# A place of its own for the second half of batch 1's v, loaded together with the first half

## The chip, the cores and the metric

The kernel runs on one core of one Trainium2 chip. The metric is the device time of one execution in microseconds (us), as the median of several runs; a profile records one execution more closely, engine by engine: PE (TensorE, matrix products), DVE (VectorE), ACT (ScalarE), POOL (GpSimd, which here mostly issues weight loads) and SP (SyncE, which issues the other loads and the stores).

## The reference

The inputs are q, k and v of 8 batches, 8 heads, 576 rows, 64 columns, and two weight matrices. A linear attention (softmax of q over its columns, softmax of k over the sequence) is followed by two matrix products with a gate between:

```
q_s = softmax(q, axis=-1);  k_s = softmax(k, axis=2)
kv  = einsum('bhsd,bhse->bhde', k_s, v)
x   = einsum('bhsd,bhde->bhse', q_s, kv)      -> 4608 x 512
h   = x @ w_in                                # 512 x 2048
g   = h * erf(softplus(h))
out = g @ w_out                               # 2048 x 512
```

The weights arrive as 64-bit floats, are read as 32-bit integers, and are decoded by shifts and masks on DVE.

## The kernel before, in words

**Tiling.** Two batches make a pair of 1152 tokens, which is cut into three blocks of 384 tokens. For each block and each of four groups of 512 hidden columns there is a work item n: up-matmuls (`mm1_32` for the first six items, in 32-bit; `mm1` later, with operands split into two 16-bit parts), softplus and erf on ACT, the multiplication `gmul` on DVE, and out-matmuls `mm2` on PE that accumulate over the groups. In the profile the up-matmuls of the first items are line L1031 (banks pX, pY, pZ), the first out-matmuls L1109 (o), the later ones L992 and L1118.

**Attention.** `attention(b)` is a generator for batch b, from batch 1 on; the order string `ORDER` and later `pace` take its pieces (token A) between the pieces of the work items. For one batch: maximum of k and its transposes (kT L524, kB L539), exponentials of k and q (L349), then two products `kv_mm(b, 0)` and `kv_mm(b, 1)` (L560, the name kv), one for each half of four heads. Each multiplies a half of k with the same half of v, and with the 64 tail rows of k and v (`kt`, `vtail`). A column of ones beside v gives the sum of k's exponentials, and `kv_norm` (L580 to L583) divides by it on DVE. `kv_max` (L589) takes the largest value, which PE turns (x_bk, L125) and DVE reduces (x_e, L127) to a scale. Then come the normalisation of q, its transposes (qT, L657) and the product x (L675).

**Where v lies.** `vbuf` holds one half of v, of four heads. `load_kv(b)` loads both halves of k, and the first half of v into vbuf, then `vtail`; for b > 0 the second half is loaded into the same vbuf (L415, called in `attention` at L714), once `kv_mm(b, 0)` has read it. SP issues its DMAs strictly in its written order, so whatever stands behind one that waits, waits too. Batch 0 is treated by itself in `start`: its second half of v lies in a buffer of the work items (tag G).

**Where the weights lie.** `WT` is a list of eight places, one for each slab of w_in or w_out in the order of `JOBS`. In the end a place holds the split 16-bit operands; for w_in it has 7168 16-bit columns. Before that, the first 4096 columns of a place serve as a landing place of raw weight pieces (`wload`, L188) and as the place of a decoded slab (`wdecode`, L214 shift, L217 and L220 or). WT[0], the first place for w_in's operands, is a landing place again and again until all pieces are decoded; its split operands are written by `wsplit(0)` (token S0), after the pieces of batch 1's attention. The first eight raw pieces are issued by SP, the other eight by POOL, each when DVE's last decoding step of an older piece has freed the landing place (rw or WT[0], WT[1]).

The written order is that in which the code calls things; the layer that records the program then places each engine's instructions, and may let some pass others. The order of the program on each engine, as it was built, is what the rows of order below show.

Of the kernel before, what the change touches and what calls it, by code (L numbers as in the profile page):

```python
# [9 lines left out]
F32 = mybir.dt.float32  # L10
# [46 lines left out]
def attn_moe_kernel(  # L57
# [9 lines left out]
    nc = tc.nc  # L67
    B, H, S, D = q.shape
# [4 lines left out]
    TM = 4  # L73
# [41 lines left out]
    WT = [  # L115
        cp.tile([P, 2 * (7 if which == "in" else 4) * 512], F16, name=f"wt{i}")
        for i, (which, g) in enumerate(JOBS)
    ]
# [283 lines left out]
    def load_half(src, tag, b, hf):  # L402

        s4 = src[b, hf * 4:hf * 4 + 4, 0:SM, :].rearrange("h (p t) d -> p h t d", t=TM)
        if tag == "v" and b == 0 and hf == 1:
            t = ch.tile([P, 4, TM, D + 1], F32, tag="G", bufs=2, name=f"v_{b}_{hf}")
            nc.gpsimd.memset(t[:, :, :, D:], 1.0)
        elif tag == "v":
            t = vbuf
        else:  # L410
            t = at.tile([P, TM, 4, D], F32, tag=tag, name=f"{tag}_{b}_{hf}")
        eng = nc.sync
        for h in range(4):
            o = 2 * (h % 2) + h // 2 if tag == "q" else h
            eng.dma_start(t[:, h, :, :D] if tag == "v" else t[:, :, o, :], s4[:, h])  # L415
        return t
# [9 lines left out]
    def load_tail(src, tag, p):  # L426
        t = at.tile([P, H, D], F32, tag=tag, bufs=1, name=f"{tag}_{p}")
        for j in range(2):
            nc.sync.dma_start(
                t[j * TAIL:(j + 1) * TAIL],  # L430
                src[2 * p + j, :, SM:S, :].rearrange("h p d -> p h d"),
            )
        return t

    def load_vtail(b):

        j = b % 2
        own, rest = (slice(i * TAIL, (i + 1) * TAIL) for i in (j, 1 - j))
        nc.gpsimd.memset(vtail[rest], 0.0)
        nc.gpsimd.memset(vtail[own, :, D:], 1.0)  # L440
        nc.sync.dma_start(
            vtail[own, :, :D], v[b, :, SM:S, :].rearrange("h p d -> p h d")
        )
# [10 lines left out]
    def rows(t):  # L454
        return t.rearrange("p t h d -> p (t h) d")

    def q_sub(t, g, name):

        m = at.tile([P, g], F32, tag=f"qm{g}", bufs=1, name=f"{name}_m")
        nc.vector.tensor_reduce(m, t, axis=AX.X, op=ALU.max)  # L460
        nc.vector.tensor_tensor(
            t, t, m[:, :, None].to_broadcast([P, g, D]), op=ALU.subtract
        )
# [23 lines left out]
    def load_kv(b):  # L487
        d = bat[b]
        d["k"] = [load_half(k, "k", b, hf) for hf in range(2)]
        if b % 2 == 0:  # L490
            d["kt"] = load_tail(k, "kt", b // 2)
        d["v"] = [load_half(v, "v", b, 0)]
        load_vtail(b)

    def load_q(b, hf):
# [12 lines left out]
    def k_max(b, ks, kt):  # L508

        kmax = asc[:, 0].rearrange("p (h d) -> p h d", h=H)  # L510
        k2 = asc[:, 1].rearrange("p (t h d) -> p t h d", t=2, h=4)
        for hf in range(2):
            nc.vector.tensor_tensor(k2, ks[hf][:, 0:2], ks[hf][:, 2:4], op=ALU.max)
            nc.vector.tensor_tensor(
                kmax[:, hf * 4:hf * 4 + 4, :], k2[:, 0], k2[:, 1], op=ALU.max
            )
        nc.vector.tensor_tensor(kmax[kt[1]], kmax[kt[1]], kt[0], op=ALU.max)
        return kmax

    def k_max_T(b, kmax):  # L520
        bk = bank(f"kT_{b}")
        km2 = hd(kmax)
        for c in range(NC4):
            nc.tensor.transpose(  # L524
                bk[:, c * P:(c + 1) * P], km2[:, c * P:(c + 1) * P], ident
            )
        km = at.tile([P, NC4], F32, tag="km", bufs=1, name=f"km_{b}")
        nc.vector.tensor_reduce(
            km, bk.rearrange("p (c s) -> p c s", c=NC4), axis=AX.X, op=ALU.max
        )  # L530
        return km
# [155 lines left out]
    def attention(b):  # L687
        d, j, p = bat[b], b % 2, b // 2
        even = bat[b - j]
        tl = slice(j * TAIL, (j + 1) * TAIL)  # L690
        ks, qs, kt = d["k"], d["q"], even["kt"][tl]
        kmax = k_max(b, ks, (kt, tl))
        yield SHARES[0]
        km = k_max_T(b, kmax)
        q_sub(rows(qs[0]), 16, f"q_{b}_0")
        yield SHARES[1]
        kb = k_max_rows(b, km)
        for hf in range(2):
            nc.vector.tensor_tensor(
                ks[hf], ks[hf],  # L700
                kb[:, None, hf * 4:hf * 4 + 4, :].to_broadcast([P, TM, 4, D]),
                op=ALU.subtract,
            )
        nc.vector.tensor_tensor(kt, kt, kb[tl], op=ALU.subtract)
        yield SHARES[2]
        q_sub(rows(qs[1]), 16, f"q_{b}_1")
        if j == 1:
            q_sub(even["qt"], H, f"qt_{p}")
        yield SHARES[3]
        for t in (*ks, kt, qs[0], qs[1], *([even["qt"]] if j == 1 else [])):  # L710
            act(t, t, AF.Exp, chain=b > 1)
        yield SHARES[4]
        kv_norm(b, 0, kv_mm(b, 0))
        d["v"].append(load_half(v, "v", b, 1))  # L714
        q_norm(rows(qs[0]), 16, f"q_{b}_0", b)
        yield SHARES[5]
        if b >= QDMA:
            q_turn_half(b, 0)
        kv_norm(b, 1, kv_mm(b, 1))
        if b + 1 < B:  # L720
            load_kv(b + 1)
        mx = kv_max(b)
        yield SHARES[6]
        kv_split(b, mx)
        yield SHARES[7]
        q_norm(rows(qs[1]), 16, f"q_{b}_1", b)
        if b >= QDMA:
            q_turn_half(b, 1)
        if j == 1:
            q_norm(even["qt"], H, f"qt_{p}", b, asc[:, 1] if b < QDMA else None)  # L730
            if b >= QDMA:
                q_turn_tail(p)
        yield SHARES[8]
        for i in ((3 * p + 1, 3 * p + 2) if j else (3 * p, 3 * p + 1)):
            while not x_free(i):
                yield 0

        def tails():
            if b < QDMA:
                bk = bank(f"qTt_{p}")  # L740
                for c in range(NC4):
                    nc.tensor.transpose(
                        bk[:, c * P:(c + 1) * P], asc[:, 1, c * P:(c + 1) * P], ident
                    )
                even["qtT"] = q_evac(b, 0, bk)
            yield SHARES[9]
            qT = even["qtT"]
            bks = [bank(f"xt_{p}_{a}") for a in range(2)]
            x = xblock(p * NBK + 1)
            for j_ in range(2):  # L750
                for hf in range(2):
                    oc = slice(hf * P + j_ * TAIL, hf * P + (j_ + 1) * TAIL)
                    qs_ = [
                        qT[:, :, (2 * hf + c) * P + j_ * TAIL:(2 * hf + c) * P + (j_ + 1) * TAIL]
                        for c in range(2)
                    ]
                    x_mm(2 * p + j_, hf, [bk[:, oc] for bk in bks], qs_)
            w = TAIL if b < E32 else P
            for a, bk in enumerate(bks):
                bk3 = bk[:, :2 * P].rearrange("p (f s) -> p f s", f=2)  # L760
                for j_ in range(P // w):
                    o = SM - T + j_ * TAIL
                    x_put(
                        bk3[:, :, j_ * TAIL:j_ * TAIL + w], x[:, a::2, o:o + w],
                        bat[j_]["sx"] if b < E32 else None,
                    )
            if b + 1 < B:
                bat[b + 1]["qt"] = load_tail(q, "qt", p + 1)
            yield SHARES[10]

        if j == 1 and b < QDMA:
            yield from tails()
        for hf in range(2):
            if hf == 1 and j == 1 and b >= QDMA:
                yield from tails()
            qTs = []
            for c in (2 * hf, 2 * hf + 1):
                qTs.append(q_T(b, c, bank(f"qT_{b}_{c}")) if b < QDMA else d["qT"][c])
                if b < QDMA and c % 2 == 1 and b + 1 < B:
                    load_q(b + 1, hf)  # L780
                yield SHARES[11]
            bks = [bank(f"x_{b}_{hf}_{a}") for a in range(2)]
            x_mm(b, hf, bks, qTs)
            if b >= QDMA and b + 1 < B:
                load_q(b + 1, hf)
            for a in range(2):
                x_split(b, 2 * hf + a, bks[a])
            if hf == 1:
                d["xdone"] = True
            yield 2 * SHARES[12]  # L790
# [480 lines left out]
```

## Time and profile before

| | |
|---|---|
| runs | 844.3, 844.45, 847.89 us |
| median | 844.45 us |
| profiled execution | 847.55 us |
| its span | 845.3 us, 15526 instructions |
| granted TensorE clock, mean of the span | 0.996 |
| busy: PE, DVE, ACT, POOL | 815.5, 624.3, 504.1, 15.8 us |
| moved by DMA | 61.55 MB |

A row of a timeline gives the start in us, the length in us, the engine, the line of the kernel, the operation, what it writes and reads, and how many records are merged in it; in brackets stands how long the engine was idle before it and what ended that. A 32-bit matmul of the program is two records. A row of the chain gives start, length, engine and line of one piece of the chain of work that ended last. A row of the table by stretches gives the busy time of each engine (with instructions in brackets), the granted TensorE clock as a share of full speed, the mean busy share of the DMA engines, and GB/s. A row of DMA issues gives the size of one transfer and the median time in us from issue to landing. DVE's busy rows can overlap a little where one instruction starts while the last one drains.

### The profile page before, as it was taken

Reading aid. Unit: us, or ns where it says so; the run is one execution under the profiler, and the core shown is the slowest. Engines: PE = TensorE matmul, PEld = TensorE weight load, DVE = VectorE, ACT = ScalarE, POOL = GpSimd, SP = SyncE. Lnnn points to the kernel's source line nnn. Section 1 sums busy time; section 2 is a strip of 40 time slices with the busy share of each in tenths; the row PEclk is TensorE's granted clock in tenths of the full one; section 3 lists DMA queues with packets and bytes.
Section 4 is the critical chain, followed back from the end, with each engine's and each line's share of the span. In section 5 each row is a group of like instructions: output and inputs, shape, how many; then the busy total and the mean of one; then the engine's idle time right before and its main releaser. Section 6 shows DMA issues by size and latency. Waiting matters only on the chain.

```text
span 845.3 us, 15526 instructions
## 1 busy us (share of the span) xinstructions
PE 815.5 (96%) x6546; PEld 549.7 (65%) x6546; DVE 624.3 (74%) x887; ACT 504.1 (60%) x645; POOL 15.8 (2%) x36
## 2 busy tenths in 40 slices
PE   5997999999999999999999999999999999999997
PEld 4554545666667666766776676766776676777672
DVE  6999689998898768857876769856876557553543
ACT  3787459877574757565764467465665465544532
POOL 2101000000000000000000000000000000000000
PEclk9999999999999999999999999999999999999999
DMA  9976721032227303511171113411140100000100
GB/s 258 408 192 185 196 50 38 1 74 59 63 50 143 90 1 76 119 26 27 54 152 34 58 24 76 112 33 26 38 76 14 38 2 1 38 2 1 38 2 37
DMA packets 141348, 61.55 MB, mean 73 GB/s; under 512 B 130528, under 2 KB 132576, under 8 KB 141280
## 3 DMA queue, kind: packets, MB, share of 16 engines
q1 hardware_dynamic: 139104, 52.18, 25.0%
q0 software_dynamic: 2176, 8.39, 2.8%
q8 instruction: 51, 0.84, 0.4%
q14 instruction: 17, 0.14, 0.1%
HBM read 45.09 MB, written 9.44 MB: 65 GB/s over the span
## 4 chain that ended last, share of the span: by engine, by line
PE 62%; DVE 16%; ACT 11%; DMA 5%; SPq 3%; issue 3%; ACTq 0%; DVEq 0%
PE o L1118 26%; PE pX L992 14%; PE pZ L992 7%; ACT G L349 4%; ACT L349 4%; PE o L1109 3%; PE pY L992 3%; DVE G L1072 3%; DMA q<-in_q_dram 2%; PE pX L1031 2%; SPq L415 2%; DVE H L1090 2%; PE kv L560 2%; DVE x L301 1%; DVE H L1086 1%
## 5 line engine op out<-in xcount | busy, mean ns | idle before, releaser
L1118 PE MATMUL o<-wt,H 128*128 128x512 f16 x1512 | 347.2, 379 | 1.7 <-DVE H L1086 1.3
L992 PEld LDWEIGHTS <-wt 128*128 128x128 f16 x3528 | 294.6, 98 | 37.9 <-issue 16.1
L1118 PEld LDWEIGHTS <-H 128*128 128x128 f16 x1512 | 145.9, 98 | 150.9 <-DVE H L1086 1.8
L992 PE MATMUL pX<-x,wt 128*128 128x192 f16 x2016 | 195.1, 247 | 6.8 <-DVE H L1014 3.2
L349 ACT ACT_TABLE_LOAD x104 | 133.4, 1283 | 8.3 <-DVE H L1017 6.2
L1072 DVE SCALAR_TENSOR_TENSOR G<-G,small,H 128x1536 f32<-128x1536 f32 x44 | 79.9, 1817 | 55.1 <-ACT G L349 55.0
L1019 ACT COPY H<-pX 128x384 f32<-128x384 f32 x42 | 20.0, 475 | 139.9 <-PE pX L992 137.4
L992 PE MATMUL pZ<-x,wt 128*128 128x192 f16 x1008 | 98.4, 246 | 0.0
L349 ACT ACTIVATE G<-H,U 128x768 f32<-128x768 f32 (+1 forms) x56 | 69.2, 1253 | 22.1 <-DVE H L1017 21.5
L1090 DVE TENSOR_TENSOR H<-G,H 128x1536 f16<-128x1536 f32 x42 | 73.7, 1755 | 0.8
L349 ACT ACTIVATE G<-G 128x1536 f32<-128x1536 f32 x48 | 71.2, 1484 | 0.5
L992 PE MATMUL pY<-x,wt 128*128 128x192 f16 x504 | 49.4, 249 | 0.0
L449 ACT ACTIVATE x<-x 128x384 f32<-128x384 f32 (+1 forms) x52 | 16.2, 396 | 48.4 <-PE x L675 48.4
L1004 DVE COPY H<-pY 128x384 f32<-128x384 f32 x42 | 23.2, 553 | 28.0 <-PE pY L992 28.0
L300 ACT ACTIVATE x<-x 128x768 f16<-128x768 f32 (+1 forms) x44 | 33.0, 765 | 16.1 <-DVE x L393 16.0
L1017 DVE TENSOR_TENSOR H<-pZ,H 128x384 f32<-128x384 f32 x42 | 23.2, 552 | 26.3 <-PE pZ L992 26.2
L1086 DVE CAST H<-G 128x1536 f16<-128x1536 f32 x42 | 40.2, 957 | 0.8
L301 DVE SCALAR_TENSOR_TENSOR x<-x,x 128x768 f16<-128x768 f32 (+1 forms) x44 | 37.3, 851 | 3.2 <-ACT x L300 3.2
L1134 DVE TENSOR_SCALAR ob<-o,V 128x512 f32<-128x512 f32 x29 | 21.7, 748 | 20.4 <-PE o L1118 20.4
L1031 PE MATMUL pX<-x,wt 128*128 128x384 f32 x96 | 34.0, 488 | 0.0
L1006 DVE TENSOR_TENSOR H<-pX,H 128x384 f32<-128x384 f32 x42 | 23.3, 555 | 14.1 <-PE pX L992 13.2
L460 DVE TENSOR_REDUCE q_m<-q 128x16 f32<-128x1024 f32 x14 | 17.0, 1216 | 19.7 <-DMA q<-in_q_dram 19.7
(180 smaller groups left out, 822.1 us busy)
## 6 DMA issues: line engine op xcount, KB each, us to landing
out_dram<-ob SPq DMA_DIRECT2D x32, 256.0 KB, 2.3
vbuf<-in_v_dram SPq DMA_DIRECT2D x60, 128.0 KB, 3.3
q<-in_q_dram SPq DMA_DIRECT2D x56, 128.0 KB, 3.1
k<-in_k_dram SPq DMA_DIRECT2D x56, 128.0 KB, 3.2
wt<-in_moe_w_out_dram POOLq DMA_DIRECT2D x5, 1024.0 KB, 6.5
wt<-in_moe_w_in_dram SPq DMA_DIRECT2D x4, 1024.0 KB, 12.2
wt<-in_moe_w_out_dram SPq DMA_DIRECT2D x2, 1024.0 KB, 15.9
H_raw<-in_k_dram SPq DMA_DIRECT2D x2, 512.0 KB, 4.6
```

What stands on the lines that cost most here:

```text
L300: nc.scalar.activation(hi, src, AF.Copy, scale=s)
L301: nc.vector.scalar_tensor_tensor(lo, src, s, hi, op0=ALU.mult, op1=ALU.subtract)
L349: i = nc.scalar.activation(out_, in_, func, **kw)
L992: nc.tensor.matmul(o, w[wl][:, c, a * P:(a + 1) * P], x[:, xl, xi, c, :], start=(new and a == 0 and c == 0 and i == 0), stop=(c == 1 and i ...
L1004: nc.vector.tensor_copy(C[0, 0], bank2("Y"))
L1006: add(C[0, 0], bank2("X"), C[0, 0], op=ALU.add)
L1031: nc.tensor.matmul(ph[:, :T], w[:, c, a * P:(a + 1) * P], x[:, c, :], start=(c == 0), stop=(c == NC4 - 1),)
L1072: nc.vector.scalar_tensor_tensor(flat(s["G"]), flat(s["G"]), GA32 if n < N32 else GA[:, g:g + 1], flat(s["H"]), op0=ALU.mult, op1=ALU.mult,)
L1086: nc.vector.tensor_copy(flat(s["gh"]), flat(s["G"]))
L1090: nc.vector.tensor_tensor(flat(s["gl"]), flat(s["G"]), flat(s["gh"]), op=ALU.subtract)
L1109: nc.tensor.matmul(o, s["G"][:, a, ts_], w[:, a, :], start=(first_ and a == 0), stop=(last_ and a == FG - 1),)
L1118: nc.tensor.matmul(o, s[gt][:, a, ts_], w[wl][:, a, :], start=(first_ and a == 0 and i == 0), stop=(last_ and a == FG - 1 and i == 2),)
```

## The change

The second half of batch 1's v no longer goes to vbuf. It gets 2080 of the upper 16-bit columns of WT[0] (from 4096 on, 1040 32-bit values for each partition: four heads, four rows, 64 columns and the one of ones), which no raw piece uses. `load_kv(1)` loads both halves, and `attention(1)` no longer loads the second. The ones column there is set by a memset on POOL. Batches 2 to 7 stay as they were.

```
@@ load_half
             t = ch.tile([P, 4, TM, D + 1], F32, tag="G", bufs=2, name=f"v_{b}_{hf}")
             nc.gpsimd.memset(t[:, :, :, D:], 1.0)
+        elif tag == "v" and b == 1 and hf == 1:
+
+            t = WT[0][:, 4096:4096 + 8 * TM * (D + 1)].bitcast(F32)
+            t = t.rearrange("p (h t e) -> p h t e", h=4, t=TM)
+            nc.gpsimd.memset(t[:, :, :, D:], 1.0)
         elif tag == "v":
             t = vbuf
@@ load_kv
-        d["v"] = [load_half(v, "v", b, 0)]
+        d["v"] = [load_half(v, "v", b, hf) for hf in range(1 + (b == 1))]
         load_vtail(b)
@@ attention
         kv_norm(b, 0, kv_mm(b, 0))
-        d["v"].append(load_half(v, "v", b, 1))
+        if b > 1:
+            d["v"].append(load_half(v, "v", b, 1))
```

On PE, in batch 1's attention (kv_1_0 and kv_1_1 are its two kv products, o_0_2 an out-matmul's bank, x1_bk the turned maximum), the order of before is:

```order
L560 MATMUL kv_1_0_560<-vbuf_82,k_1_0_352 64x65 x8
L560 MATMUL kv_1_0_560<-vtail_84,kt_0_104 64x65 x2
L1109 MATMUL o_0_2_498<-wt6_95,G_1_457 128x512 x2
L560 MATMUL kv_1_1_594<-vbuf_82,k_1_1_357 64x65 x8
L560 MATMUL kv_1_1_594<-vtail_84,kt_0_104 64x65 x2
L1109 MATMUL o_0_2_498<-wt6_95,G_1_457 128x512
L560 MATMUL kv_1_1_594<-vbuf_82,k_1_1_357 64x65 x8
L560 MATMUL kv_1_1_594<-vtail_84,kt_0_104 64x65 x2
L1109 MATMUL o_0_2_498<-wt6_95,G_1_457 128x512
L1031 MATMUL pX_3_0_694<-x_0_136,wt7_96 128x384 x4
L125 MATMUL x1_bk_661<-ident_76,mx_1_639 128x128
```

and of the change, at the same place (line numbers above 407 are five or six higher):

```order
L565 MATMUL kv_1_0_565<-vbuf_82,k_1_0_352 64x65 x8
L565 MATMUL kv_1_0_565<-vtail_84,kt_0_104 64x65 x2
L565 MATMUL kv_1_1_595<-wt0_89,k_1_1_357 64x65 x8
L565 MATMUL kv_1_1_595<-vtail_84,kt_0_104 64x65 x2
L565 MATMUL kv_1_1_595<-wt0_89,k_1_1_357 64x65 x8
L565 MATMUL kv_1_1_595<-vtail_84,kt_0_104 64x65 x2
L1115 MATMUL o_0_2_503<-wt6_95,G_1_462 128x512 x4
L1037 MATMUL pX_3_0_695<-x_0_136,wt7_96 128x384 x4
L125 MATMUL x1_bk_662<-ident_76,mx_1_640 128x128
```

The second kv product reads WT[0] and stands directly behind the first; the four out-matmuls that stood around and between its parts stand behind it.

On SP, from batch 1's k to batch 2's q, the order of before is:

```order
L415 DMA k_1_1_357<-in_k_dram 128x4x64 x4
L415 DMA vbuf_82<-in_v_dram 128x4x64 x4
L441 DMA vtail_84<-in_v_dram 64x8x64
L415 DMA vbuf_82<-in_v_dram 128x4x64 x4
L415 DMA k_2_0_619<-in_k_dram 128x4x64 x4
L415 DMA k_2_1_624<-in_k_dram 128x4x64 x4
L429 DMA kt_1_629<-in_k_dram 64x8x64 x2
L415 DMA vbuf_82<-in_v_dram 128x4x64 x4
L441 DMA vtail_84<-in_v_dram 64x8x64
L429 DMA qt_1_759<-in_q_dram 64x8x64 x2
```

and of the change:

```order
L420 DMA k_1_1_357<-in_k_dram 128x4x64 x4
L420 DMA vbuf_82<-in_v_dram 128x4x64 x4
L420 DMA wt0_89<-in_v_dram 128x4x64 x4
L446 DMA vtail_84<-in_v_dram 64x8x64
L420 DMA vbuf_82<-in_v_dram 128x4x64 x3
L420 DMA k_2_0_620<-in_k_dram 128x4x64 x4
L420 DMA k_2_1_625<-in_k_dram 128x4x64 x4
L434 DMA kt_1_630<-in_k_dram 64x8x64 x2
L420 DMA vbuf_82<-in_v_dram 128x4x64
L446 DMA vtail_84<-in_v_dram 64x8x64
L434 DMA qt_1_760<-in_q_dram 64x8x64 x2
```

The four loads of the second half stand ahead of batch 1's vtail; behind it, three of the four loads of batch 2's first half of v have come ahead of batch 2's k.

On DVE two instructions of batch 2's tail of q (its maximum and its subtraction) stand one decode step and two earlier than before; all else on DVE, and all on ACT, keeps its order.

## The prediction

> **What bounds the kernel now.** I read the page's busy times first, then the chain that ended last around the change, then each engine's timeline there.
>
> ```profile
> PE 815.5 (96%) x6546; PEld 549.7 (65%) x6546; DVE 624.3 (74%) x887; ACT 504.1 (60%) x645; POOL 15.8 (2%) x36
> ```
>
> PE is busy 96% of the span, so time can come only from a place where PE waits, or runs slowly. Between 76 and 120 us the chain is this (start, length, what):
>
> ```profile
> 76.25 0.52 SPq L415
> ...
> 76.89 6.84 DMA vbuf<-in_v_dram
> ...
> 88.97 2.58 PE pX L1031 x8
> ...
> 119.50 0.63 PE kT L524 x4
> ```
>
> The transfer at 76.89 is the second half of batch 1's v: it goes into vbuf, so SP can issue it only when the first kv product has read vbuf. The second kv product waits for it. PE's and DVE's timelines show the two waits (in brackets: idle before the row, and what ended it):
>
> ```profile
> 77.82 0.29 PE L560 MATMUL kv<-vtail,kt 128*64 128x65 f32 x4
> 78.04 1.98 PE L1109 MATMUL o<-wt,G 128*128 128x512 f32 x4
> 83.77 0.62 PE L560 MATMUL kv<-vbuf,k 128*64 128x65 f32 x13 [3.49 <-DMA vbuf<-in_v_dram]
> 91.39 0.27 PE L125 MATMUL x_bk<-ident,mx 128*128 128x128 f32 x1
> 81.11 1.75 DVE L1069 TENSOR_TENSOR G<-G,H 128x1536 f32<-128x1536 f32 x1
> 87.80 0.16 DVE L580 TENSOR_SCALAR rd<-kv 128x2 f32<-128x2 f32 x1 [4.93 <-PE kv L560]
> 89.99 0.41 DVE L589 TENSOR_REDUCE mx<-kvh 128x1 f32<-128x256 f32 x1
> 91.70 0.29 DVE L127 TENSOR_REDUCE x_e<-x_bk 128x1 f32<-128x128 f32 x1 [0.63 <-PE x_bk L125]
> ```
>
> PE is empty for 3.49 us, and DVE, which stands in order at the normalisation of that product, for 4.93 us. PE also runs slowly afterwards; in these stretches of 4 us the third number from the end is the granted clock:
>
> ```profile
> 80.00:84.00 4.00, 0.51 (x9) 0.37 (x10) 2.87 (x3) 2.44 (x8) 0.00 (x0) 1.00 1.09 340
> 84.00:88.00 4.00, 4.00 (x41) 2.31 (x38) 0.20 (x2) 0.00 (x0) 0.12 (x1) 0.58 0.65 106
> 88.00:92.00 4.00, 4.00 (x13) 2.28 (x13) 3.37 (x10) 0.41 (x1) 0.51 (x2) 0.99 0.58 132
> ```
>
> 0.58 over 4 us and 0.99 over the next 4 lose 1.68 + 0.04 = 1.72 us of full clock.
>
> **The change, part by part.** *The wait for v.* The second half is now issued before the vtail load and has another place, so the second kv product (40 matmul records) follows the first at 77.82 + 0.29 = 78.1 us. Its price with all data there, and that of the out-matmuls behind it, come from:
>
> ```profile
> 185.36 1.32 PE kv L560 x40
> 46.56 10.46 PE L1109 MATMUL o<-wt,G 128*128 128x512 f32 x24
> ```
>
> The product ends at 78.1 + 1.32 = 79.4. Four out-matmuls of 2 records follow, 8 x 10.46/24 = 3.49, to 82.9; then the first up-matmul group, 2.58 in the chain, to 85.5, instead of 91.4. On DVE the product is ready before the G multiplication of 81.11 ends at 82.86, so the 4.93 us go in full: everything from 87.80 moves to 82.86, 4.94 earlier. The maximum, ended at 89.99 + 0.41 = 90.40, ends at 85.46, when PE is just ready to turn it (x_bk). So both engines meet without a gap to speak of: x_bk moves from 91.39 to about 85.5 (5.9 earlier), DVE's reading of it from 91.70 to no earlier than 91.70 - 0.63 - 4.94 = 86.1 (5.6 earlier), because the 0.63 us wait goes too. That is the upper end. The lower end: the stretch from 78.04 to x_bk at 91.39 is 13.35 us; without the idle 3.49 and the clock loss 1.72 it is 8.14, so x_bk at 86.2, its reader 91.70 - 91.39 = 0.31 later at 86.5: 5.2 earlier. The row sums are cleaner, but the 8.14 holds real switching between kv and out-matmuls, part of which stays; I take 5.5.
>
> *Does the gain survive to 120 us?* Each later wait of the stretch must hang on something that moves along (the last row is from the view of waits between 40 and 125 us: total, times, longest):
>
> ```profile
> 95.28 0.69 DVE L214 TENSOR_SCALAR sg<-wt 128x1024 int32<-128x1024 int32 x1
> 101.95 0.70 DVE L214 TENSOR_SCALAR rw<-wt 128x1024 int32<-128x1024 int32 x1 [3.47 <-DMA wt<-in_moe_w_out_dram]
> 113.49 1.22 DVE L460 TENSOR_REDUCE q_m<-q 128x16 f32<-128x1024 f32 x1 [1.39 <-DMA q<-in_q_dram]
> 95.66 0.71 POOL L188 DMA_DIRECT2D wt<-in_moe_w_out_dram  x1 [7.10 <-DVE sg L220]
> SPq L415 <- PE qT L657: 13.7, 2, 11.4
> ```
>
> The weight transfer that DVE wants at 101.95 is issued by POOL at 95.66, when DVE's decode (L220) has freed its place, so it moves by the same 5.5. Batch 2's q, wanted at 113.49, is issued by SP when PE's transposes (qT) have read the old q, so it moves too. From 120 us on the chain is again PE, DVE and ACT in an order that the change leaves alone, so 5.5 us earlier at 119.50 is 5.5 us at the end.
>
> *What is added.* One POOL memset of v's ones column, as long as the one of 1.95 us (0.13 us), at the start, where POOL waits for q next; POOL is busy 15.8 us in the whole span, and without that cover it would be 0.13 us. Four v loads on SP ahead of vtail:
>
> ```profile
> 1.95 0.13 POOL L407 MEMSET v<- 128x16 f32 x1
> 55.48 2.65 SPq L415 DMA_DIRECT2D vbuf<-in_v_dram  x4
> 77.19 0.34 PE L560 MATMUL kv<-vtail,kt 128*64 128x65 f32 x4
> ```
>
> The four cost SP 2.65 us; vtail goes out at 60.8 instead of 55.48 + 2.65 = 58.1 and is read first at 77.19, so 13 us or more cover its landing. SP has nothing else until 76.2. The writer of these columns in the place of w_in's operands is the split of the first w_in slab, which the written order puts behind batch 1's whole attention: no wait.
>
> *What moves.* At 76.2 SP now issues three of batch 2's first v loads where the late v loads were, and its second-half k loads no longer wait for the late product, whose reader stood at 87.80. So four more 128 KB loads share the DMA engines with the weight transfer POOL issues at 76.97:
>
> ```profile
> 76.97 0.71 POOL L188 DMA_DIRECT2D wt<-in_moe_w_out_dram  x1 [8.33 <-DVE wt L220]
> wt<-in_moe_w_out_dram POOLq DMA_DIRECT2D x1, 1024.0 KB, 6.5
> ```
>
> It lands at 76.97 + 6.5 = 83.5; half a MB more at the 340 GB/s above is 1.5 us, so 85.0 at worst. DVE reads it at 95.28, now 89.8: covered by 4.8 us. On DVE the tail of q's maximum and subtraction move two places forward, equal work. Both at nothing.
>
> Sum: the profiled execution, 847.55 (span 845.3), goes to 842.0. It stands 3.1 above the median of the runs, 844.45; taking the 5.5 from the median gives **839.0**.
>
> **The rivals.**
>
> *More is gained: a later slow stretch goes too (0.20).* The clock also falls at 306 us, after a gap of 2.05 us, and doesn't fall after one of 1.44 us:
>
> ```profile
> 305.86 1.50 PE L992 MATMUL pX<-x,wt 128*128 128x192 f16 x12 [2.05 <-DVE H L1014]
> 605.39 1.15 PE L992 MATMUL pX<-x,wt 128*128 128x192 f16 x12 [1.44 <-ACT H L1011]
> 304.00:308.00 4.00, 2.14 (x18) 2.07 (x18) 2.27 (x3) 0.59 (x2) 0.00 (x0) 0.81 0.00 0
> 308.00:312.00 4.00, 4.00 (x28) 3.08 (x27) 1.12 (x2) 3.97 (x3) 0.00 (x0) 0.76 0.02 4
> 604.00:608.00 4.00, 2.61 (x20) 1.77 (x20) 3.94 (x5) 3.44 (x5) 0.00 (x0) 1.00 0.00 0
> ```
>
> It loses 0.76 + 0.96 = 1.72 us, the same as the first stretch. A gap of 2 us is near the limit, and moved by 5.5 us it may fall differently against whatever measures it; then 839.0 - 1.7 = 837.3. Against it: two of two gaps of 2 us or more had a slow stretch. [...]
>
> *The gain is caught by the weight transfer of 101.95 (0.10).* If that transfer landed no earlier than before, because k, kt and v loads now crowd it, DVE would run as before from 101.95 and only lose its 1.39 us wait at 113.49: 843.1. For it: DVE already waits 3.47 us there. Against: its issue moves with DVE, and the SP loads move away from it, not towards it.
>
> *No change (0.04).* The second product is still held, by its bank or by a whole-tile dependency on the place of w_in's operands: 844.45. Against: the trace puts PE's wait at 83.77 down to the v transfer alone.
>
> *Slower (0.05).* The earlier k loads hold up the weight transfer of 76.97 itself. The row that bounds this is a weight load in the crowded start:
>
> ```profile
> raw<-in_moe_w_in_dram SPq DMA_DIRECT2D x1, 1024.0 KB, 25.1
> ```
>
> At 25.1 us it would land at 102.1 instead of being ready at 95.28: DVE's decode of the third w_out slab would run 6.8 us later than before, 851.3. It decides from a landing after 95.3, 18.3 us after issue, against 6.5 now. [...]
>
> **How the numbers follow.** The forecast has the rest, 0.61. About 0.5%, 4.2 us (840.2), is what a measurement of this kernel can tell from no change. The forecast's own ends are 844.45 - 5.2 = 839.3 and 844.45 - 5.9 = 838.6, so nearly all of it and the first rival lie below 840.2: faster 0.77 (a little of 0.81 is left for spread between runs). Within 0.5%: the caught gain, no change and that spread, 0.18. Slower: 0.05. The range runs from 844.45 - 5.9 - 1.7 = 836.8 to the caught gain's 843.1.
>
> **What would show it.** Right: no idle before kv from vbuf or its new place at about 78 us, DVE's L580 row with no 4.9 us wait, clock 1.00 through 84 to 92, x_bk near 85.5, the kT transposes of batch 2 near 114. Wrong: those steps moved but kT still near 119 (caught), with DVE waiting for a weight transfer for over 3.5 us; or kT near 114 and the end not moved, which would put a fixed event behind 120 us that I don't see.

## The result and the profile after

| | before | change |
|---|---|---|
| median, runs of one chip (8 each) | 844.96 us | 838.84 us |
| lowest to highest | 842.79 to 848.24 | 837.93 to 840.05 |
| profiled execution, its span | 847.55, 845.3 | 839.42, 837.6 |
| granted TensorE clock, mean of that span | 0.996 | 0.999 |
| busy PE, DVE, ACT | 815.5, 624.3, 504.1 | 811.6, 624.0, 503.9 |

The ratio is 0.9923 (95% interval 0.9905 to 0.9942): the change is faster by 0.6 to 1.0%. The forecast of 839.0 against 844.45 was a ratio of 0.9935, inside the interval.

The stretch around the change, first PE's timeline of the changed kernel:

```profile
77.52 0.29 PE L565 MATMUL kv<-vtail,kt 128*64 128x65 f32 x4
77.64 0.64 PE L565 MATMUL kv<-wt,k 128*64 128x65 f32 x16
78.11 0.29 PE L565 MATMUL kv<-vtail,kt 128*64 128x65 f32 x4
78.22 0.64 PE L565 MATMUL kv<-wt,k 128*64 128x65 f32 x16
78.69 0.29 PE L565 MATMUL kv<-vtail,kt 128*64 128x65 f32 x4
78.91 3.70 PE L1115 MATMUL o<-wt,G 128*128 128x512 f32 x8
82.44 2.74 PE L1037 MATMUL pX<-x,wt 128*128 128x384 f32 x8
85.27 0.29 PE L125 MATMUL x_bk<-ident,mx 128*128 128x128 f32 x1
113.50 0.63 PE L529 MATMUL kT<-ident,asc 128*128 128x128 f32 x4 [0.62 <-DVE asc L522]
```

The second product reads its operand in WT[0] (here wt) at 77.64, directly behind the first, and ends at 78.98; there is no bracket up to x_bk. DVE's timeline at the same place, with the two later waits that the prediction wanted to see move along:

```profile
80.83 1.78 DVE L1075 TENSOR_TENSOR G<-G,H 128x1536 f32<-128x1536 f32 x1
82.50 0.18 DVE L585 TENSOR_SCALAR rd<-kv 128x2 f32<-128x2 f32 x1
84.71 0.41 DVE L594 TENSOR_REDUCE mx<-kvh 128x1 f32<-128x256 f32 x1
85.71 0.29 DVE L127 TENSOR_REDUCE x_e<-x_bk 128x1 f32<-128x128 f32 x1
89.28 0.70 DVE L214 TENSOR_SCALAR sg<-wt 128x1024 int32<-128x1024 int32 x1
96.13 0.69 DVE L214 TENSOR_SCALAR rw<-wt 128x1024 int32<-128x1024 int32 x1 [3.63 <-DMA wt<-in_moe_w_out_dram]
107.50 1.22 DVE L465 TENSOR_REDUCE q_m<-q 128x16 f32<-128x1024 f32 x1 [1.54 <-DMA q<-in_q_dram]
130.74 1.82 DVE L1078 SCALAR_TENSOR_TENSOR G<-G,small,H 128x1536 f32<-128x1536 f32 x1
```

The waits of 4.93 and 0.63 us are gone, and those of 3.47 and 1.39 us are there again as 3.63 and 1.54, each some 6 us earlier. The last row stood at 136.73 in the kernel before, 5.99 later. The first kv product's start is already 0.31 us earlier in this execution (75.21 against 75.52), where nothing was changed; so the stretch itself won 5.68 us. The granted clock is the third number from the end of each stretch of 4 us:

```profile
80.00:84.00 4.00, 4.00 (x12) 1.96 (x11) 4.00 (x9) 2.17 (x6) 0.00 (x0) 1.00 1.11 315
84.00:88.00 4.00, 3.92 (x14) 2.08 (x13) 4.00 (x13) 0.48 (x1) 0.00 (x0) 1.00 1.09 199
88.00:92.00 4.00, 4.00 (x14) 2.41 (x13) 3.93 (x6) 2.29 (x6) 0.71 (x1) 1.00 1.03 177
300.00:304.00 4.00, 3.67 (x40) 3.32 (x40) 1.80 (x4) 2.45 (x3) 0.00 (x0) 1.00 0.01 4
304.00:308.00 4.00, 4.00 (x35) 2.97 (x34) 1.03 (x3) 3.97 (x4) 0.00 (x0) 1.00 0.00 0
```

0.58 became 1.00. The last two rows are the place of the later slow stretch, which in this execution is gone too, though its gap is as long as before (2.09 against 2.05 us):

```profile
300.33 1.15 PE L998 MATMUL pX<-x,wt 128*128 128x192 f16 x12 [2.09 <-DVE H L1020]
```

From 300 to 380 us the G multiplications show what that is worth. These are a first and a last one of this piece of the program, in the kernel before and then in the change:

```profile
299.99 1.81 DVE L1072 SCALAR_TENSOR_TENSOR G<-G,small,H 128x1536 f32<-128x1536 f32 x1
379.17 1.82 DVE L1072 SCALAR_TENSOR_TENSOR G<-G,small,H 128x1536 f32<-128x1536 f32 x1 [2.91 <-ACT G L349]
```

```profile
294.46 1.81 DVE L1078 SCALAR_TENSOR_TENSOR G<-G,small,H 128x1536 f32<-128x1536 f32 x1
371.99 1.82 DVE L1078 SCALAR_TENSOR_TENSOR G<-G,small,H 128x1536 f32<-128x1536 f32 x1 [2.77 <-ACT G L349]
```

79.18 us became 77.53: 1.65 us. So the 7.7 us between the two spans are 0.31 from ahead of the change, 5.68 from its stretch, 1.65 from the later clock, and small pieces of both signs (0.46 lost between 137 and 300 us, about 0.9 won near 589, where a gap of 1.44 us before is 0.49 after, and 0.4 lost behind the last G multiplication). The 0.9 is not the change's: a run below that keeps the late v ("The later slow stretch") has 0.85 of it too, so it doesn't hang on the change.

### The profile page after: what moved, and what is told of

It is laid out like the page before. It is cut to its first block, busy times and chain, and to the rows that moved or that the text cites. A ratio compares the mean times of both kernels' runs of the same rounds, so it can differ in the third digit from the quotient of the medians.

```text
span 837.6 us, 15532 instructions
## 1 busy us (share of the span) xinstructions
PE 811.6 (97%) x6546; PEld 547.3 (65%) x6546; DVE 624.0 (74%) x887; ACT 503.9 (60%) x645; POOL 15.9 (2%) x37
## 4 chain that ended last, share of the span: by engine, by line
PE 59%; DVE 19%; ACT 13%; DMA 4%; issue 3%; SPq 2%; ACTq 0%; DVEq 0%
PE o L1124 25%; PE pX L998 14%; PE pZ L998 6%; ACT G L349 4%; ACT L349 4%; PE pY L998 3%; DVE G L1078 3%; DVE H L1096 2%; PE o L1115 2%; SPq L420 2%; DMA q<-in_q_dram 2%; PE pX L1037 2%; PE kv L565 1%; DVE x L301 1%; PE x L680 1%
```

## The experiments

The theory: the second product was held by its place (vbuf was occupied, so its load went out late, and landed later still, in 6.2 us, beside a 1 MB weight transfer), PE's emptiness of 3.49 us then slowed the clock to 0.58, and the delay reached DVE, which stood in order at that product. The rivals: the moved loads brought it (their order on SP); or the crowd on the DMA engines alone; or the emptiness of PE and its clock alone. All runs without another word are compared with the kernel before on the same chip.

**The place, without the early call.** The change, but the load call stays where it stood, behind the first kv product:

```
@@ against the change
-        d["v"] = [load_half(v, "v", b, hf) for hf in range(1 + (b == 1))]
+        d["v"] = [load_half(v, "v", b, 0)]
...
-        if b > 1:
-            d["v"].append(load_half(v, "v", b, 1))
+        d["v"].append(load_half(v, "v", b, 1))
```

> The second half of batch 1's v has its own place as in the change, but the call that loads it stays where it was before, behind the first kv product. Theory (what counts is the place: without the dependency on vbuf SP, which has nothing else to do, issues the load behind vtail, long before 78 us): the same as the change, 838.8 us or 0.992 of before, within 1.5 us, no wait of PE for v, clock 1.00 from 84 to 92 us. Rival (what counts is that it is loaded together with the first half, in the written order): nearer to before, 843 to 845 us.

Measured: 837.82 us, ratio 0.9911 (0.9884 to 0.9939). With nothing to wait for, the four loads stand directly behind vtail on SP, early all the same, at 59.91 us (SP's order is that of the recorded program, not that of the calls); the orders of PE, DVE and ACT are those of the change. Counted from the start of the first kv product, the G multiplication near 137 us comes 5.95 us earlier than before. So the place is what counts, and the moved call brings nothing of its own that these runs can tell. The profiled execution, at 841.12 us the slowest of the five (the others took 836.76 to 837.83), has the later slow stretch again, after a shorter gap than that of the change:

```profile
300.89 1.15 PE L997 MATMUL pX<-x,wt 128*128 128x192 f16 x12 [2.00 <-DVE H L1019]
```

```profile
300.00:304.00 4.00, 3.11 (x28) 3.02 (x28) 1.58 (x4) 1.89 (x3) 0.00 (x0) 0.78 0.02 4
304.00:308.00 4.00, 4.00 (x22) 2.57 (x21) 0.83 (x2) 3.97 (x3) 0.00 (x0) 0.80 0.00 0
```

**The crowd on the DMA engines.** The kernel before, with the one weight load that POOL issues at 76.97 held back until POOL has set vtail's columns of ones, which it can do once the second product has read vtail:

```
@@ wload, against the kernel before
-            eng.dma_start(raws[i], src.rearrange("(a p) n -> p a n", p=P))
+            with tc.issue_after(tail_set[0].ins) if i == 13 else ExitStack():
+                eng.dma_start(raws[i], src.rearrange("(a p) n -> p a n", p=P))
@@ load_vtail
-        nc.gpsimd.memset(vtail[own, :, D:], 1.0)
+        tail_set[0] = nc.gpsimd.memset(vtail[own, :, D:], 1.0)
```

> The kernel before, with the late load into vbuf and its wait, but the 1 MB weight transfer that POOL issues at 77 us is issued only when the second kv product is done. Theory with a part for contention (the late v takes 6.8 us to land because it shares the DMA engines with that transfer): the v pieces land within 3.3 to 4 us, at 80 to 82.5 us, PE idles under 2 us and keeps its clock, DVE waits under 1 us instead of 4.9: 840 to 842 us (0.994 to 0.997), the rest being given back if the held transfer now lands later than DVE wants it, at about 90 us. Rival (the time to landing is the load's own): landing still 6 to 7 us, 845 us.

Measured: 842.62 us, ratio 0.9988 (0.9968 to 1.0008): above the 840 to 842 expected, and in the interval not apart from the kernel before. The group of DMA issues of the four late v loads, in the kernel before and in this one:

```profile
vbuf<-in_v_dram SPq DMA_DIRECT2D x4, 128.0 KB, 6.2
```

```profile
vbuf<-in_v_dram SPq DMA_DIRECT2D x4, 128.0 KB, 3.1
```

and this kernel's waits, on PE, on DVE, and the held load on POOL:

```profile
84.26 0.62 PE L562 MATMUL kv<-vbuf,k 128*64 128x65 f32 x13 [0.50 <-DMA vbuf<-in_v_dram]
86.89 0.16 DVE L582 TENSOR_SCALAR rd<-kv 128x2 f32<-128x2 f32 x1 [0.83 <-PE kv L562]
87.60 0.71 POOL L189 DMA_DIRECT2D wt<-in_moe_w_out_dram  x1
101.19 0.69 DVE L216 TENSOR_SCALAR rw<-wt 128x1024 int32<-128x1024 int32 x1 [3.78 <-DMA wt<-in_moe_w_out_dram]
107.69 0.69 DVE L216 TENSOR_SCALAR rw<-wt 128x1024 int32<-128x1024 int32 x1 [3.29 <-DMA wt<-in_moe_w_out_dram]
84.00:88.00 4.00, 3.74 (x43) 2.30 (x44) 3.17 (x9) 1.95 (x6) 0.97 (x3) 1.00 0.73 164
```

Without that transfer beside them the v loads land in half the time, 3.1 us instead of 6.2, so half of the late landing was that transfer; the two waits shrink from 3.49 and 4.93 to 0.50 and 0.83 us, and the clock stays at 1.00. The profiled execution is the slowest of the twelve (848.27 us): another slow stretch, after a gap of 2.48 us at 68 us, lies ahead of the held load in it (four up-matmul records at 68.95 took 2.76 us, as long as eight elsewhere, 2.74), so times are counted from the first product. The turn of the maximum (x_bk) comes 4.54 us earlier; at 137 us 2.53 are left. The held load itself lands in 6.0 us, at 93.6, and the next one in 6.6 us, much as before (6.3). The one after that, issued at 97.71, takes 10.0 us instead of 6.5, and DVE waits 3.29 us for it, where it waited for none before. Why it took so long isn't shown; the held load had landed by then. So this way some 2 of the 4.5 us are given back to a weight transfer.

**PE kept busy through the wait.** The kernel before, with the four out-matmuls ahead of the second product and ten extra matmuls behind them, whose bank nothing reads; v still comes late:

```
@@ attention, against the kernel before
         kv_norm(b, 0, kv_mm(b, 0))
+        if b == 1:
+            r = kv32[1][:, 0:2, :].rearrange("p c e -> p (c e)")
+            fl = psh.tile([P, 512], F32, tag="pZ", name="fill")
+            for _ in range(10):
+                fill[0] = nc.tensor.matmul(fl[:, :128], ident, r, start=True, stop=True)
@@ kv_mm: the first matmul of kv_mm(1, 1)
+                    with tc.issue_after(fill[0].ins) if first else ExitStack():
```

> The kernel before, with the late load and its wait, but PE is kept busy in it: all four out-matmuls stand ahead of the second kv product, and ten extra 32-bit matmuls into an unused bank fill the rest. Theory (of the gain, a part is the slow clock after the gap and the out-matmuls that come after the product; the rest is the late data): clock 1.00 from 84 to 92 us, the product ends near 85.1 instead of 87.6 us, DVE waits about 2.3 instead of 4.9 us: 2.6 us gained, 842.3 us or 0.997. Rival (only the data's arrival counts, the clock and the order on PE cost nothing): no change, 845 us. If the slow clock were the whole cost: 839 us.

Measured: 838.59 us, ratio 0.9927 (0.9903 to 0.9950), as good as the change, where 842.3 was expected. The expectation failed, and DVE's timeline shows why:

```profile
84.02 0.16 DVE L469 TENSOR_SCALAR qt_r<-qt_r 128x8 f32<-128x8 f32 x1
84.09 0.69 DVE L214 TENSOR_SCALAR sg<-wt 128x1024 int32<-128x1024 int32 x1
84.70 0.19 DVE L472 RECIPROCAL qt_r<-qt_r 128x8 f32<-128x8 f32 x1
85.05 0.16 DVE L583 TENSOR_SCALAR rd<-kv 128x2 f32<-128x2 f32 x1 [0.15 <-PE kv L563]
```

The layer that records the program had also placed the normalisation of q and a part of the weights' decoding ahead of the normalisation that waits. So DVE waits 0.15 us instead of 4.93, with v as late as ever. So this run changed two things at once, PE's emptiness and DVE's order, and couldn't tell one from the other.

**The same, with DVE's order as before.** The order is held by three conditions more (q's reciprocal behind the first instruction of the waiting normalisation, the sum of q's tail behind its reciprocal, the decode behind the maximum), so that DVE again stands at the second product first, and keeps the order of before up to x_e:

```
@@ against the run with the filled wait
-        nc.vector.reciprocal(r, r)
+        with ExitStack() if o_ != 0 else tc.issue_after(rds[0].ins):
+            nc.vector.reciprocal(r, r)
...
+        with ExitStack() if o_ != 1 else tc.issue_after(rds[1].ins):
...
+        with tc.issue_after(rds[2].ins) if i in (12, 13) else ExitStack():
```

> The kernel before, with the ten extra matmuls and the four out-matmuls ahead of the second kv product as in the run with the filled wait, but with DVE's order held to that of before: the normalisation of the second product stands ahead of the decode of w_out. The extra matmuls write a bank that nothing reads. Theory (PE's wait counts only as far as it delays DVE, which stands in order at that normalisation): clock 1.00 from 84 to 92, the product ends near 85.3 instead of 87.8, so DVE waits about 2.4 us instead of 4.93, kT of batch 2 comes 2.5 us earlier, and the time is 841.8, ratio 0.997. Rival 1 (the filled PE alone brought the 5.7 us of the run with the filled wait, not DVE's order): 838.6, ratio 0.993. Rival 2 (only the landing of v counts, and clock and order are worth nothing): 844.3, ratio 1.000.

Measured: 841.11 us, ratio 0.9964 (0.9947 to 0.9981). PE's and DVE's timelines, and the clock:

```profile
82.09 2.40 PE L725 MATMUL fill<-kvh,ident 128*128 128x128 f32 x20
84.42 0.69 PE L567 MATMUL kv<-vbuf,k 128*64 128x65 f32 x16
85.99 0.16 DVE L587 TENSOR_SCALAR rd<-kv 128x2 f32<-128x2 f32 x1 [2.61 <-PE kv L567]
```

```profile
84.00:88.00 4.00, 4.00 (x52) 3.02 (x51) 2.01 (x6) 0.00 (x0) 0.63 (x2) 1.00 1.12 195
```

With the clock at 1.00 and the out-matmuls already done, DVE's wait falls by 2.3 us to 2.61, and the time by about 3. That is about half of the change's gain; the rest is the 2.61 us for which DVE still waits. So both halves of the theory stand: the empty PE cost the clock (0.58 behind the wait of 3.49 us, 1.00 with it filled), and DVE's place in order made the wait count. The run with the held weight load parts the clock from the out-matmuls, since there PE kept its old order at a clock of 1.00. From PE's restart on v to DVE's normalisation it is 4.03 us in the kernel before (83.77 to 87.80), 2.63 there (84.26 to 86.89) and 1.57 here (84.42 to 85.99): an estimate from these rows of about 1.4 us for the clock and 1.1 for the out-matmuls in between.

**The loads of batch 2.** The change, with all of batch 2's k and v loads moved behind the load of q's tail, so that they crowd nothing at 76 us:

```
@@ attention, against the change
-        if b + 1 < B:
+        if b + 1 < B and b != 1:
             load_kv(b + 1)
@@ behind qt's load for batch 2
+            if b == 1:
+                with tc.issue_after(tail_dma[0].ins):
+                    load_kv(2)
```

> The change, but batch 2's loads of k and of the first half of v, which the change lets SP issue from 76 us on, stand behind the load of the tail of q, at 88 us or later, as late as before or later. Theory (the gain is the removed wait of PE and DVE; these loads are wanted only at about 110 us): as the change, 838.8 us within 1 us, at most 1.5 us more if they crowd the weight transfer issued at 90 us. Rival (a good part of the gain comes from these loads no longer standing behind the late v on SP): 842 us or more.

Measured: 838.79 us, ratio 0.9930 (0.9905 to 0.9955): nothing against the change. The order of these loads on SP didn't bring the gain, and the median shows no cost of it. (In this profile DVE now waits up to 2.02 us for batch 2's q, whose loads stand behind the moved ones, and the G multiplication near 137 us comes 0.4 us later after the first product than in the change.)

**The later slow stretch.** Sixteen extra 16-bit matmuls, whose bank nothing reads, in the gap near 300 us, first in the kernel before, then in the change:

```
@@ mm1, k == 3
             add(C[0, 1], bank2("Z"), C[0, 1], op=ALU.add)
+            if n == 14:
+                fl = psh.tile([P, 512], F32, tag="pY", name="fill")
+                w = wop(jn, 0, 4, 1)[:, 0]
+                for _ in range(16):
+                    nc.tensor.matmul(
+                        fl[:, :Th], w[:, 0, :P], x[:, 0, 2, 0, :], start=True, stop=True,
+                    )
             prod("X", 2, 4)
```

> The kernel before, with 16 extra 16-bit matmuls of 192 columns in the gap of 2.05 us that stands at 303.8 to 305.9; they write a bank that nothing reads. At the length of the matmuls around them, 1.15 us for 12, they take 1.5 us and leave 0.5. Theory (the slow stretch after that gap comes from PE's idleness and costs 1.7 us): clock 1.00 from 304 to 312, the piece between the first G multiplications near 300 and near 379 at 77.5 instead of 79.2, and a median of 842.6 if every execution of the kernel before has the stretch, up to 843.8 if only some do (their mean clocks go from 0.994 to 0.999); ratio 0.998 to 0.9995. Rival 1 (the clock falls there for another reason): stretch stays, 844.3. Rival 2 (the extra matmuls delay the product behind them): 1 us or more slower, 845.3.

> The changed kernel, with the same 16 extra matmuls in the same gap, which stands near 300 there. Theory (the gap of the changed kernel mostly falls so that no slow stretch follows, as in its profile): no change against it, 838.8, at most 0.3 us less. Rival 1 (it has the stretch as often as the kernel before, and the profile was luck): 837.5. Rival 2 (the extra matmuls cost what they take): 840.0 or more.

Measured on the kernel before: 843.25 us, ratio 0.9987 (0.9974 to 1.0001). Its gap and its clock there:

```profile
304.82 1.15 PE L992 MATMUL pX<-x,wt 128*128 128x192 f16 x12 [0.42 <-DVE H L1014]
```

```profile
304.00:308.00 4.00, 3.58 (x42) 3.33 (x41) 1.80 (x5) 1.96 (x3) 0.00 (x0) 1.00 0.02 4
```

The slow stretch is gone and the piece from 298.96 to 376.48 takes 77.52 us, as in the change, instead of 79.18. In the median that is 1.1 us, whose interval still holds no change, which fits that not every execution of the kernel before has the stretch: over 51 of them the mean clocks go from 0.993 to 1.000, and 0.002 of a span of 842 is one such stretch.

Measured on the change: 837.52 us, ratio 0.9923 (0.9898 to 0.9948). Five of its six executions took 836.6 to 838.6, one 842.61, and that one was profiled. It shows no slow clock near 300 us but something else, the group of the weight transfer that POOL issues at 89.59 (6.5 us in the change), and what waited for it on DVE and PE:

```profile
wt<-in_moe_w_out_dram POOLq DMA_DIRECT2D x1, 1024.0 KB, 9.5
```

```profile
99.12 0.69 DVE L214 TENSOR_SCALAR rw<-wt 128x1024 int32<-128x1024 int32 x1 [6.71 <-DMA wt<-in_moe_w_out_dram]
106.75 1.91 PE L680 MATMUL x<-asc,kvh 64*64 64x512 f32 x8 [3.73 <-ACT asc L652]
108.00:112.00 4.00, 4.00 (x10) 1.59 (x8) 4.00 (x4) 3.33 (x9) 0.00 (x0) 0.59 0.00 0
```

The transfer lands 3 us late, qt behind it lands late too, PE stands empty for 3.73 us, and the clock falls to 0.59. The next weight transfer is late in turn: the median of the five of that group is 9.5 us there, 6.5 in the change (where this one took 6.1). By 137 us nearly the whole gain is gone (135.58 against 136.73 before, of which 0.37 is an earlier first product): the rival of the caught gain, in one execution of six.

**The change once more, and both edits together.** To settle whether the extra matmuls help the change, it ran again beside the first kernel of this list (place, without the early call) with the sixteen matmuls:

> The changed kernel, unaltered, beside its version with the 16 extra matmuls near 304 us, on the same chip. Theory (in most executions its 2 us gap brings no slow stretch, so that the extra matmuls have little to win): 838.8, ratio 0.993, at most 0.3 us above the version with the extra matmuls. Rival (the 837.5 of that version was a gain of 1.3 us, since the change still loses a slow stretch in many executions): 838.8, and the version with the extra matmuls 1.0 us or more below it.

> The place of its own for v with the load call left behind the first product, which had 837.8 and a slow stretch in its profile, and the 16 extra matmuls near 304 us. Theory (the stretch is all that its profiled execution lost): 837.5, ratio 0.992, no slow stretch at 304 to 312. Rival (the extra matmuls bring nothing, or the order of the loads brings the 1 us to the change): 838.8, ratio 0.9935. If a weight transfer of w_out lands late, as in the profile of the change with the extra matmuls, single executions stand 4 to 5 us higher in both kernels.

Measured: the change 838.54 us, ratio 0.9921 (0.9892 to 0.9950), highest 839.52; the other 837.86 us, ratio 0.9913 (0.9886 to 0.9939), clock 1.00 at 296 to 312. No execution of either stands as high as the 842.61 us of the late weight transfer. The 0.7 us between them lie within the spread of either (837.22 to 839.52, and 836.42 to 839.28), and the two kernels differ in the load call too, so whether the extra matmuls are worth anything beside the change isn't settled; in these runs it is about 1 us at most (837.52 on another chip with them, 838.54 without).

## Why the prediction was right, step by step

- **The wait for v: right.** The second product was to follow at 78.1 and end at 79.4, the out-matmuls at 82.9, the first up-matmuls at 85.5, x_bk at about 85.5; measured 77.64, 78.98, 82.61, 85.18 and 85.27, with the 0.31 us of an earlier start in each. DVE's reading of x_bk was to come no earlier than 86.1, and came at 85.71; with the 0.31 counted back that is 0.1 earlier than the bound, as DVE's rows overlap there (the one ahead ends at 85.11 + 0.69 = 85.80, 0.09 later).
- **The size: 5.5 forecast, 5.7 in the profile.** It lies between the two row sums on PE (5.2, which leaves the switching between products in, and 5.9), just above that on DVE (5.6). That the time itself met the forecast within 0.2 us (838.84 against 839.0) is partly luck: the median before is 844.96 in the runs that were compared, not the 844.45 it was counted from, and the gain in the median is 6.1. The four parts, 3.49 of idleness and 1.72 of clock on PE, 4.93 and 0.63 on DVE, are two views of one gain and rightly weren't added: with the clock and PE's order mended alone, 2.61 us of DVE's wait stayed, and the time lay between.
- **The gain survives: right.** The G multiplications from 137 to 265 us all stand 6.0 us earlier. Both waits moved along, for the reasons given: POOL's issue of the weight load went from 95.66 to 89.66, and SP's issue of q with PE's transposes.
- **What was added: nothing, as said.** The memset took 0.12 us at 1.95; SP's four loads took 2.65 us and vtail went out at 60.66 (60.8 forecast), and the first product didn't wait for it.
- **What moved: nothing.** The weight load of 76.66 landed in 6.6 us, where up to 8 were allowed, and DVE read it at 89.28 without a wait. With those loads moved away the time stayed.
- **The rival of the later clock (0.20): probably too small a chance.** It came true in the profiled execution, in which the stretch is gone; in the median its part can't be told. "Two of two gaps of 2 us or more had a slow stretch" was two samples. In the three profiles of the unaltered change and the place alone there is one slow stretch after a gap of 2.00, and none after gaps of 2.09 and 1.63. Over all runs that give a clock, the kernel before has a mean of 0.9968 in 51 executions, the change 0.9993 in 14: a difference of 0.0025, which in 842 us is 2.1 us. Of the 51, 24 lose 0.004 or more, which is two stretches; of the 14, 13 lose at most 0.001. How much of this belongs to the first stretch and how much to the later one isn't known: ten of the 51 lose at most 0.001, so the first stretch isn't in all of them either. Those ten have a median of 842.3, the 13 of the change 838.5, so some 3.8 us are gained even where no slow stretch shows on either side.
- **The caught gain (0.10): a real mechanism, but a rare one.** It was seen in one execution (of the change with the sixteen matmuls), at 842.61 us against the 843.1 worked out for it, with PE's wait of 3.73 us and a slow stretch that the forecast didn't have; and none of the 14 executions of the unaltered change comes near that. Why the transfer took 9.5 us there isn't known.
- **Slower (0.05) and no change (0.04)** are out: nothing was held by the whole tile, and the weight load of 76.66 stayed far from the 18.3 us at which it would have counted.

What stays open is the small change: the gap near 300 us was 0.69 to 2.09 us long in these kernels, though nothing was changed there, and why a weight transfer of POOL now and then takes 9.5 us (in the change with the extra matmuls) or 10.0 (in the run with the held weight load) instead of about 6.5 wasn't followed further.

## What to carry to other kernels

Where one buffer serves two loads in a row, ask which engine stands in order at the second consumer. Here the waits on that engine, DVE, were 4.93 and 0.63 us, and the stretch won 5.68 when a place of its own for the data removed them; with other work ahead of the waiting instruction, and PE filled, 0.15 of the 4.93 were left. Holding back the transfer that crowds it won only a part of it here: the load landed in half the time (3.1 us instead of 6.2), but a later transfer then took longer (10.0 instead of 6.5). An idle stretch of the tensor engine like these is to be priced with the slow clock: it followed six of the seven gaps of 2 us or more listed below, at a cost of 1.65 to 1.72 us where that was measured.

## What the runs showed of the hardware

- After a gap of PE of about 2 us the clock sometimes fell and sometimes didn't, not by length alone: it fell after 2.05, 2.00 and 1.99 us (the last in the run with the held weight load), to 0.76, 0.78 and 0.62 in the slowest stretch of 4 us, and not after 2.09 and 1.75 (1.00 in the stretches behind them), nor after 1.91, where a pair of out-matmul records 1.2 us behind the gap took 1.02 us, against 1.97 in the slow clock after 3.49 us. Behind PE's first matmul it fell after each of the longer gaps seen (2.48, 3.19, 3.49 and 3.73), to 0.58 to 0.64 after the last three. One such stretch cost 1.65 to 1.72 us. That a gap moved by some us may fall differently was the author's estimate: no run here shifted a gap alone, and what decides besides the length isn't shown.
- Four loads of 128 KB landed in 3.1 us without a weight transfer beside them (the run with the held weight load), and in 6.2 beside one of 1 MB (the kernel before), at the same place of the program.
- Runs of the kernel before spread over 8 us (841.39 to 849.59 in 51 executions), those of the change over 2.8 (837.22 to 840.05 in 14). The ten runs of the kernel before with a mean clock of 0.999 or more have a median of 842.3, the 24 with 0.996 or less 845.4.
